# Keys projected first, their features turned to rows by DMA as pairs of float16, and the recall one block later

## The chip, the cores and the metric

The kernel runs on one core of a Trainium2 chip. The metric is the device time of that core in microseconds (us). TensorE (PE) multiplies matrices; ScalarE (ACT), VectorE (DVE) and GpSimd (POOL) work element by element; SyncE (SP) issues the DMA transfers. Each engine goes through its own instructions strictly in order, and waits where an input or a buffer isn't ready.

## What is computed

```python
o = g_beta * a_mem + (1 - g_beta) * a_dot      # per head, 32 heads of 18, 4 segments of 512 tokens
a_mem = phi(q) @ M / (phi(q) @ z + 1e-6)       # phi(t) = t + 1 if t > 0 else exp(t)
M = M + phi(k).T @ v ;  z = z + phi(k).sum()   # after each segment
a = o @ wo                                     # a_dot: causal softmax attention in the segment
b = (gelu(x @ w_gate) * (x @ w_up)) @ w_down   # 576 -> 4608 -> 576
out = g * a + (1 - g) * b                      # g = sigmoid(x . gate_w); x is 2048 x 576
```

## The kernel before

**Numbers as pairs.** A float32 operand is split into a high and a low float16 word with a common scale, and a product is three float16 matmuls (high by high, high by low, low by high). Making a pair takes one ACT instruction for the high words and one DVE instruction for the low words: lines L109 and L112 for weights, L170 and L175/L180 for x.

**Stages.** The first stage projects x to queries, keys and values, and forms what the memory M adds. It goes through four segments s = 0 to 3. Then come 72 steps of the feed-forward part, with the attention's products among them, and last the output projection. The order of PE, ACT, DVE and POOL is the order in which the program is written, inside one block of manual scheduling; only SP's queue is ordered by the framework.

**Columns.** In each segment `project` (L460 to L466) makes nine blocks of 128 columns by 512 tokens in PSUM, each from 14 matmuls of 512 columns (`chain_w`, L322 to L325). The blocks 0 to 4 hold queries and 4 to 8 keys, so block 4 holds both. `put_columns` (L468 to L491) stands one block later in the program: ACT writes the block's high words to `stage` (L470). Where phi is wanted, ACT also makes relu and exp (L475, L476), DVE the other half of phi (L480), and POOL adds the two (L481). DVE writes the low words (L486), and a DMA stores the pair (L487). Four PSUM buffers take the blocks in turn, and `stage` has three buffers. In segment 0 phi is only wanted of the keys, blocks 4 to 8; in segment 3 only of the queries.

**What stands beside the columns.** `beside_products` (L737) puts other work between the blocks. In segment 0 these are the projection weights: block j makes the pair `wp` of block j + 2 and, to j = 4, a part of the values' weights `wv`. In segments 0 to 2 `next_x` prepares the x of the segment after it: squares on ACT at j = 2 and 3, their sum on PE at j = 4 (`scale_x`, L155, with six small DVE steps, L157 to L164, that end in `xis`), six small POOL steps with the scales that follow from it (`outscale`, L120 to L127), then the high words at j = 5 to 7 and the low words at j = 6 to 8.

**Rows.** From segment 1 on, the nine blocks are preceded by four blocks q of 128 tokens. `vrows` makes the values (`chain_x`, L332 to L335, from x and `wv`), ACT evicts them twice (float16 pairs L506, and float32 with a column of ones, `v32`, L508), and DVE makes the low words (L511). Between them lies the memory's part of the segment before, p = s - 1. `key_rows` (L566) turns phi of the keys to rows by six float32 transposes on PE (L571, L573) and two ACT evictions (L575, L576). `memorize` (L578) then multiplies those rows with `v32` in five float32 matmuls (L585) that add up in PSUM over the four blocks, and `keep_memory` (L588) adds the masked sum to `bd`. `recall` (L533) multiplies phi of the queries with `bd` in five float32 matmuls (L540).

**Tail.** `out_step` (L1364, L1369) makes the output projection from pairs that POOL prepares (L1357), in a written order of steps (L1458 and below); u counts pairs of 128-token blocks.

Of the kernel before, what the change touches and what calls it, by code (L numbers as in the profile page):

```python
# [18 lines left out]
P = 128  # L19
D = 576  # L20
F = 4608
H = 32
# [21 lines left out]
def kernel(ctx: ExitStack, tc: tile.TileContext, xs, wqk, wv, wo, wgu, wd, beta, out):  # L44
# [355 lines left out]
    with tc.tile_pool(name="prj", bufs=2, side="right", reuse_waits="tile") as pp:  # L400
        al = pp.tile([P, 4, 2], F32, name="al", bufs=1)
        nal = pp.tile([P, 4], F32, name="nal", bufs=1)
        usc = pp.tile([P, 1], F32, name="usc", bufs=1)
        mp = stay.enter_context(tc.tile_pool(name="ffn", bufs=2, reuse_waits="tile"))
# [5 lines left out]
        W, phi, vst, v32, kr, mem = {}, {}, {}, {}, {}, {}  # L410
        QG = ((0, 1), (2, 3), (4, 5), (6, 7), (8,))
# [5 lines left out]
        def load_qk(g):  # L417
            js = QG[g]
            a, b = js[0], js[-1] + 1
            sp.dma_start(raw_qk[:, a:b], wqk[a:b].rearrange("j p k n -> p j (k n)"))  # L420
# [39 lines left out]
        def project(s, j):  # L460
            w = W[j]
            i = j % 4
            pr = bank("G") if i == 0 else bank("U") if i == 3 else bank("st", 2)
            chain_w(pr, lambda k, a: w[:, a, k * P : (k + 1) * P], x16[s])
            return s, j, pr

        def put_columns(s, j, pr):
            hf, c = divmod(s, 2)  # L468
            st = pp.tile([P, 2, L], F16, name="stage", bufs=3)
            act.activation(st[:, 0], pr, AF.Copy, scale=2.0**-14)  # L470
            with_phi = (j <= 4 and s >= 1) or (j >= 4 and s <= 2)
            if with_phi:
                e = pp.tile([P, L], F32, name="expm", bufs=2)
                f = phi[s, j] = pp.tile([P, L], F32, name="phi", bufs=9)
                act.activation(e, pr, AF.Relu, scale=nal[:, s : s + 1])  # L475
                act.activation(e, e, AF.Exp, scale=-1.0)  # L476

            def rest():
                if with_phi:
                    dve.tensor_scalar(f, pr, al[:, s, 0:1], 0.0, OP.mult, OP.max)  # L480
                    (dve if j == 8 and s == 0 else pool).tensor_tensor(f, f, e, OP.add)  # L481
# [8 lines left out]
            if j == 8 and s < 3:  # L490
                held.append(words)  # L491

        def put_rows(s, q, b, pv, unit, a):

            hf, c = divmod(s, 2)
            t = 4 * c + q
            if b == 0:
                st = vst[s, q] = pa.tile([P, H, VC], F16, name="vstage", bufs=4)
                pool.memset(st[:, :, VC - 1 : VC], 1.0)
                if s <= 2:  # L500
                    v32[s, q] = pa.tile([P, H, MC], F32, name="v32", bufs=6)
                    pool.memset(v32[s, q][:, :, DH:], 1.0)
# [3 lines left out]
            act.activation(st[:, hs, 0:DH], p3, AF.Copy, scale=unit)  # L506
            if s <= 2:
                act.activation(v32[s, q][:, hs, 0:DH], p3, AF.Copy, scale=a)  # L508

            def rest():  # L510
                dve.scalar_tensor_tensor(st[:, hs, DH : 2 * DH], p3, unit, st[:, hs, 0:DH], OP.mult, OP.subtract)  # L511
# [54 lines left out]
        def key_rows(s, q):  # L566
            ka, kb = bank("st", 2), bank("V")
            tok = slice(q * P, (q + 1) * P)

            for i in range(4):  # L570
                pe.transpose(ka[:, i * P : (i + 1) * P], phi[s, 4 + i][:, tok], ident)  # L571
            for i, j in ((0, 8), (1, 4)):
                pe.transpose(kb[:, i * P : (i + 1) * P], phi[s, j][:, tok], ident)  # L573
            k = kr[s, q] = pa.tile([P, KT * P], F32, name="krow", bufs=2)
            act.activation(k[:, :448], ka[:, 64:], AF.Copy)  # L575
            act.activation(k[:, 448:], kb[:, :192], AF.Copy)  # L576

        def memorize(s, q):  # L578
            if q == 0:
                mem[s] = bank("U"), bank("pv")  # L580
            k, v = kr.pop((s, q)), v32.pop((s, q))
            for j, (a, w) in enumerate(SPANS):
                h0, h1 = HEADS[j]
                o = mem[s][j // 3][:, (j % 3) * 8 * MC : (j % 3) * 8 * MC + (h1 - h0) * MC]
                pe.matmul(o, k[:, a : a + P], v[:, h0:h1].rearrange("p h d -> p (h d)"),  # L585
                          start=q == 0 and j % 3 == 0, stop=q == 3 and j in (2, 4), skip_group_check=True)

        def keep_memory(s):  # L588
            ka, kb = mem.pop(s)
            n = 8 * MC  # L590
            for o, d, k in ((ka[:, : 3 * n], flat(bd[:, 0:3]), flat(bdm[:, 0:3])),
                            (kb[:, :n], bd[:, 3], bdm[:, 3]),
                            (kb[:64, n : n + n // 2], bd[:64, 4, : n // 2], bdm[:64, 4, : n // 2])):
                if s == 0:
                    dve.tensor_tensor(d, o, k, OP.mult)
                else:
                    m = pa.tile([P, KT * P], F32, name="krow", bufs=2)[: o.shape[0], : o.shape[1]]
                    dve.tensor_tensor(m, o, k, OP.mult)
                    dve.tensor_tensor(d, d, m, OP.add)
# [8 lines left out]
        with tc.manual_schedule(engines=ORDERED):  # L608
# [35 lines left out]
            ident = pp.tile([P, P], F32, name="ident", bufs=1)  # L644
            bd = pp.tile([P, KT, 8 * MC], F32, name="bd", bufs=1)
            pool.memset(bd[64:, KT - 1], 0.0)
            make_identity(nc, ident)
# [40 lines left out]
            def next_x(c, j):  # L688
# [6 lines left out]
                if j == 4:  # L695
                    scale_x(c)
                    for i in range(2):
                        outscale(c, i)
                if 5 <= j < 8:
                    high_x(c, j - 5)  # L700
# [37 lines left out]
            def beside_products(s, j):  # L738
                if s == 0:
                    if j < 7:  # L740
                        make_qk(j + 2)
                    if j == 1:
# [3 lines left out]
                        outscale(0, 1)  # L746
                    if j < 5:
# [46 lines left out]
            for s in range(4):  # L794
                p = s - 1
                if s:
                    for q in range(4):
# [6 lines left out]
                        if q:  # L804
                            key_rows(p, q - 1)
# [5 lines left out]
                        if p >= 1:  # L811
                            recall(p, q)
# [5 lines left out]
                    key_rows(p, 3)  # L818
# [37 lines left out]
    with tc.tile_pool(name="keep", bufs=2, side="right", reuse_waits="tile") as kp, ExitStack() as tail:  # L856
# [560 lines left out]
        with tc.manual_schedule(engines=ORDERED):  # L1417
# [39 lines left out]
            for u in range(NT):  # L1457
                if u + 2 < NT:  # L1458
                    steps = (0, 6), (1, 7), (1, 1), (0, 5), (1, 4), (1, 2), (0, 3)
                elif u + 1 < NT:  # L1460
                    steps = (0, 6), (1, 7), (1, 1), (0, 5), (1, 6), (0, 3)
                else:
                    steps = (0, 2), (0, 5), (0, 4), (0, 3)
                for i, p in steps:
                    out_step(u + i, p)
                    if u == NT - 1:
                        if p == 2:
                            store(2 * u, 0)
# [4 lines left out]
                        if p == 3:  # L1473
                            store(2 * u, 1)
                if u + 1 < NT:
# [48 lines left out]
```

## Time and profile before

| | |
|---|---|
| time, median of 3 runs | 1579.53 us (1579.09 to 1580.05) |
| the profiled execution's time | 1579.74 us |
| its span, first to last instruction | 1577.9 us |
| busy: PE / PE weight loads | 1571.2 us (100%) / 936.7 us (59%) |
| busy: DVE / ACT / POOL | 1134.3 (72%) / 1175.1 (74%) / 1210.6 us (77%) |
| first stage: columns of segment 0 | 26.25 to 54.54 us |
| rows and columns of segment 1 | 54.54 to 75.47 to 104.95 us |
| rows and columns of segment 2 | 104.95 to 130.31 to 159.79 us |
| rows and columns of segment 3 | 159.79 to 185.33 to 218.63 us |

The starts of the stages are those of PE's first instruction in each. A timeline's row has its start, its time from the first start to the last end of the instructions it groups, the engine, the line, the operation with output and inputs, the shape and the count, and in brackets the idle time ahead of it with what ended it. Where instructions are pipelined, the start of the next row and not the end of this one says how long a row held its engine.

### The profile page before, as it was taken

To read this page: it belongs to the slowest core of one execution; us is meant where nothing else is said; L and a number is where in the kernel's file an instruction comes from. 1 tells how busy PE (TensorE), PEld (TensorE's weight loads), DVE (VectorE), ACT (ScalarE), POOL (GpSimd) and SP (SyncE) were. 2 spreads that over 40 slices of the span, in tenths; PEclk is the share of its full clock that TensorE was granted. 3 is DMA by queue.
4 is the path that set the end of the run, shared out by engine and by line. 5 is a ranking of instruction groups with operands and counts; after the bars stand their busy time and mean duration, and the time that the engine had idled before them with its cause. 6 is when DMAs were issued, how large, how long until landed. Compare 5 with 4: busy or idle time off the path is not lost.

```text
span 1577.9 us, 32595 instructions
## 1 busy us (share of the span) xinstructions
PE 1571.2 (100%) x11864; PEld 936.7 (59%) x11864; DVE 1134.3 (72%) x2974; ACT 1175.1 (74%) x1996; POOL 1210.6 (77%) x1173
## 2 busy tenths in 40 slices
PE   9999999999999999999999999999999999999998
PEld 6666754555555555555555555555555555555576
DVE  6677784777777777777777777777777777776565
ACT  6666444888888888888888888888888888886421
POOL 3233756788888888898987888887879797788697
PEclk9999999999999999999999999999999999999999
DMA  6532442688888798979887899889898888774653
GB/s 243 199 125 87 140 136 75 103 130 127 130 136 137 126 141 138 137 123 141 127 137 128 136 132 138 134 133 151 132 138 129 143 128 138 128 130 86 136 112 129
DMA packets 472680, 209.87 MB, mean 133 GB/s; under 512 B 427672, under 2 KB 437400, under 8 KB 472008
## 3 DMA queue, kind: packets, MB, share of 16 engines
q1 hardware_dynamic: 472520, 207.80, 73.7%
q8 instruction: 93, 1.52, 0.4%
q14 instruction: 67, 0.55, 0.1%
HBM read 91.87 MB, written 27.26 MB: 75 GB/s over the span
## 4 chain that ended last, share of the span: by engine, by line
PE 91%; POOL 4%; ACT 2%; DVE 2%; issue 0%; DMA 0%; POOLq 0%; ACTq 0%; DVEq 0%
PE dn L1007 25%; PE U L1047 17%; PE V L1047 12%; PE G L1047 12%; PE pv L962 4%; PE U L1054 2%; PE st L322 2%; PE dn L332 2%; PE G L322 1%; PE V L1059 1%; PE G L1059 1%; PE st L915 1%; PE G L1054 1%; PE V L1054 1%; POOL pairg L1339 1%; PE U L322 1%
## 5 line engine op out<-in xcount | busy, mean ns | idle before, releaser
L942 POOL TENSOR_TENSOR ph<-pf,ph 128x512 f16<-128x512 f32 (+1 forms) x256 | 354.0, 1405 | 173.2 <-ACT ph L941 173.2
L1007 PE MATMUL dn<-paird,hh 128*128 128x288 f16 x3396 | 476.3, 286 | 0.0
L1047 PEld LDWEIGHTS <-pairg 128*128 128x128 f16 x3024 | 285.5, 98 | 304.1 <-issue 18.1
L1007 PEld LDWEIGHTS <-hh 128*128 128x128 f16 x3456 | 332.1, 98 | 153.4 <-issue 18.2
L1015 DVE SCALAR_TENSOR_TENSOR acc<-dn,ev,acc 128x288 f32<-128x288 f32 x534 | 274.2, 514 | 54.1 <-PE dn L1007 44.0
L931 ACT ACTIVATE pf<-pf,mb,esc 128x512 f32<-128x512 f32 (+3 forms) x512 | 292.9, 642 | 7.0 <-POOL ph L942 0.4
L1047 PE MATMUL U<-xt,pairg 128*128 128x512 f16 x864 | 210.0, 379 | 0.0
L1047 PE MATMUL G<-x,pairg 128*128 128x512 f16 x864 | 209.9, 379 | 0.0
L1034 POOL TENSOR_TENSOR hh<-gl,hh 128x512 f16<-128x512 f32 x144 | 164.5, 1163 | 18.4 <-ACT hh L1033 18.4
L303 POOL TENSOR_TENSOR pairg<-raw,pairg 128x640 f16<-128x640 f32 (+2 forms) x144 | 174.4, 1235 | 5.1 <-ACT pairg L299 5.1
L299 ACT ACTIVATE pairg<-raw 128x640 f16<-128x640 f32 (+2 forms) x144 | 89.9, 650 | 113.2 <-POOL raw L293 65.3
L941 ACT ACTIVATE ph<-pf 128x512 f16<-128x512 f32 (+1 forms) x256 | 172.4, 720 | 0.0
L1192 DVE COPY gl<-U 128x512 f32<-128x512 f32 x72 | 49.8, 692 | 167.2 <-POOL hh L1034 150.3
L918 DVE CUSTOM_DVE_ANT_0 pf<-st,mask 128x512 f32<-128x512 f32 (+1 forms) x256 | 157.1, 614 | 0.0
L268 POOL TENSOR_SCALAR raw<-raw,sc 128x640 f32<-128x640 f32 x72 | 136.0, 1902 | 0.0
L918 DVE CUSTOM_DVE_ANT_0 pf<-dn,mask 128x256 f32<-128x256 f32 (+1 forms) x192 | 67.1, 375 | 82.7 <-PE dn L915 82.1
L1037 ACT ACTIVATE gl<-gl,sc 128x512 f32<-128x512 f32 x144 | 96.6, 715 | 37.1 <-DVE gl L1215 19.3
L1047 PE MATMUL V<-xt,pairg 128*128 128x512 f16 x432 | 105.7, 381 | 0.0
L1047 PE MATMUL U<-x,pairg 128*128 128x512 f16 x432 | 105.0, 379 | 0.0
L1047 PE MATMUL V<-x,pairg 128*128 128x512 f16 x432 | 104.8, 378 | 0.0
L1033 ACT ACTIVATE hh<-gl 128x512 f16<-128x512 f32 x144 | 82.6, 616 | 16.4 <-DVE gl L1029 16.3
L962 PEld LDWEIGHTS <-pt 128*128 128x128 f16 x2560 | 83.4, 96 | 6.3
(305 smaller groups left out, 2642.6 us busy)
## 6 DMA issues: line engine op xcount, KB each, us to landing
raw<-in_wgu_dram SPq DMA_DIRECT2D x36, 640.0 KB
rawd<-in_wd_dram SPq DMA_DIRECT2D x36, 288.0 KB
qt<-qk SPq DMA_DIRECT2D x132, 72.0 KB
kt<-qk SPq DMA_DIRECT2D x132, 72.0 KB
qk<-stage SPq DMA_DIRECT2D x36, 256.0 KB
qt<-qk SPq DMA_DIRECT2D x132, 36.0 KB
kt<-qk SPq DMA_DIRECT2D x132, 36.0 KB
vp<-vstage SPq DMA_DIRECT2D x16, 296.0 KB
```

The costliest lines, as they stand in the source:

```text
L268: pool.tensor_scalar(r, r, scl[f // 2][0][:, 0:1], None, OP.mult)
L303: pool.tensor_tensor(spot(f, *p, 1), raw_g[f][:, p[0] : p[1]], spot(f, *p, 0), OP.subtract)
L918: dve.tensor_tensor_reduce(prob[a][:, COL[qi] : COL[qi + 1]], out[qi], mask[:, L - (qi + 1) * P :], 1.0, -3e38, OP.add, OP.max, mx[a][:, q ...
L931: act.activation(r, r, AF.Exp, bias=b[:, qi : qi + 1], scale=esc[:, 0, c : c + 1])
L941: act.activation(h[:, 0, cols], p[:, cols], AF.Copy)
L942: pool.tensor_tensor(h[:, 1, cols], p[:, cols], h[:, 0, cols], OP.subtract)
L962: pe.matmul(ov, pr[:, 10 * i + COL[qi] // P + kb], v[:, 4 * e + kb, c0 : c0 + VC], start=kb == 0 and i == 0, stop=kb == qi and i == 1)
L1007: pe.matmul(o[:, :NH], hh[:, a, q * P : (q + 1) * P], w[:, b, n * NH : (n + 1) * NH], start=i == 0, stop=i == 5)
L1015: dve.scalar_tensor_tensor(av, o[:, :NH], ev, av, OP.mult, OP.add)
L1034: pool.tensor_tensor(hh[:, 1], t, hh[:, 0], OP.subtract)
L1037: act.activation(t, o, AF.Gelu_apprx_tanh, scale=scl[f // 2][0][:, 2 + c : 3 + c])
L1047: pe.matmul(o, w[:, i, (a + k) * P : (a + k + 1) * P], x[:, b + k], start=start and k == 0 and i == 0 and b == h, stop=k == 1 and i == 1, ...
```

## The change

Everything but the tail's order lies in the first stage.

- **Keys first.** `JO` sets the order of the blocks to 4, 5, 6, 7, 8, 0, 1, 2, 3, in segments 0 to 2; the weights' loads are grouped to match. Segment 3 keeps queries first.
- **Scaled features.** New `key_scales` makes per-segment factors from the outscale, with five POOL steps and one DVE step that POOL waits for. It stands behind `outscale` at j = 4 (for segment 0 at j = 1). For the key blocks 5 to 8 phi is formed scaled: DVE's half takes the scaled factor, and a new POOL instruction multiplies the exp half by it, ahead of the add.
- **Pairs.** New `key_pairs` makes `kpair` of each key block, one block later: an ACT copy to float16 and a POOL subtraction (for block 4 an ACT copy with a scale and a DVE instruction). Two DMA transposes of 128 x 512 from SP write each pair to `krows`, 30 in all.
- **Memorize in float16.** `key_rows` (72 PE transposes, 24 ACT evictions) and `v32` (24 ACT evictions and its memsets) are gone. `memorize` takes 15 float16 matmuls of 76 to 152 (or 72 to 144) columns a block in place of 5 in float32, with the values' own pairs; their low words stand ahead of the high ones now. `keep_memory` takes nine small DVE steps a segment in place of three to six.
- **Recall one block later**, the last one beside the first columns. Buffers: phi 9 to 7, `vstage` 4 to 6.
- **Tail.** In the last two rounds steps that don't need the latest pair come ahead of those that do.

```diff
+        JO = (4, 5, 6, 7, 8, 0, 1, 2, 3)
+        QG = ((0, 1), (2, 3), (4,), (5, 6), (7, 8))
...
+        def key_scales(s):
+            m = kfz[:, s : s + 1]
+            v = pp.tile([P, 1], F32, name="kv", bufs=2)
+            pool.tensor_scalar(m, al[:, s, 0:1], 2.0**30, 1.0, OP.mult, OP.max)
+            dve.tensor_scalar(v.bitcast(I32), m.bitcast(I32), EXP, None, OP.bitwise_xor)
+            pool.tensor_scalar(kf[:, s : s + 1], v, 2.0**13, None, OP.mult)
+            pool.tensor_scalar(kal[:, s : s + 1], kf[:, s : s + 1], al[:, s, 0:1], None, OP.mult)
+            pool.tensor_scalar(kfd[:, s : s + 1], m, al[:, s, 1:2], None, OP.mult)
+            pool.tensor_scalar(m, m, 2.0**-14, None, OP.mult)
...
+        def key_pairs(s, j):
...
+            if j == 4:
+                kr[s] = pa.tile([P, 2, 4, KT * P], F16, name="krows", bufs=1)
+                act.activation(h[:, 0], f, AF.Copy, scale=kf[:, s : s + 1])
+                dve.scalar_tensor_tensor(h[:, 1], f, kf[:, s : s + 1], h[:, 0], OP.mult, OP.subtract)
+            else:
+                act.activation(h[:, 0], f, AF.Copy)
+                pool.tensor_tensor(h[:, 1], f, h[:, 0], OP.subtract)
+            for i in range(2):
+                sp.dma_start(kr[s][:, i, :, (j - 4) * P : (j - 3) * P], h[:, i], transpose=True)
...
                 act.activation(e, e, AF.Exp, scale=-1.0)
+            if to_rows:
+                key_pairs(*to_rows.pop(0))
...
-                    dve.tensor_scalar(f, pr, al[:, s, 0:1], 0.0, OP.mult, OP.max)
-                    (dve if j == 8 and s == 0 else pool).tensor_tensor(f, f, e, OP.add)
-                if j < 8 or s == 3:
+                    keys = j > 4
+                    dve.tensor_scalar(f, pr, kal[:, s : s + 1] if keys else al[:, s, 0:1], 0.0, OP.mult, OP.max)
+                    if keys:
+                        pool.tensor_scalar(e, e, kf[:, s : s + 1], None, OP.mult)
+                    pool.tensor_tensor(f, f, e, OP.add)
+                    if j >= 4 and s <= 2:
+                        to_rows.append((s, j))
...
             for j, (a, w) in enumerate(SPANS):
                 h0, h1 = HEADS[j]
-                pe.matmul(o, k[:, a : a + P], v[:, h0:h1].rearrange("p h d -> p (h d)"),
+                for n, (i, c) in enumerate(((0, DH), (1, DH), (0, 0))):
+                    pe.matmul(o[:, :, :DH] if c == 0 else o, k[:, i, 64 + a : 64 + a + w],
+                              v[:, h0:h1, c : c + MC if c else DH],
...
                 elif u + 1 < NT:
-                    steps = (0, 6), (1, 7), (1, 1), (0, 5), (1, 6), (0, 3)
+                    steps = (0, 6), (1, 1), (0, 5), (1, 2), (0, 3)
                 else:
-                    steps = (0, 2), (0, 5), (0, 4), (0, 3)
+                    steps = (0, 6), (0, 7), (0, 5), (0, 4), (0, 3)
```

ACT in the columns of segment 0, before: from the third block on to the fifth. `stage` is a block's high words, `wp` and `wv` are weights' high words, `pairg` takes the squares of the next segment's x, and G, U and st are PSUM buffers.

```order
L149 ACTIVATE pairg<-raw 128x512 x3
L470 ACTIVATE stage<-st 128x512
L109 ACTIVATE wp<-acc,wsc 128x640
L109 ACTIVATE wv<-acc,wsc 128x578
L149 ACTIVATE pairg<-raw 128x512 x2
L470 ACTIVATE stage<-U 128x512
L109 ACTIVATE wp<-acc,wsc 128x640
L109 ACTIVATE wv<-acc,wsc 128x578
L470 ACTIVATE stage<-G 128x512
```

The same engine after, from the fourth block on; L496 is the new copy of the block ahead to float16, and the last rows lie beside the fifth block.

```order
L504 ACTIVATE stage<-U 128x512
L509 ACTIVATE expm<-U,nal 128x512
L510 ACTIVATE expm<-expm 128x512
L496 ACTIVATE kpair<-phi 128x512
L109 ACTIVATE wp<-acc,wsc 128x640
L109 ACTIVATE wv<-acc,wsc 128x578
L504 ACTIVATE stage<-G 128x512
L509 ACTIVATE expm<-G,nal 128x512
L510 ACTIVATE expm<-expm 128x512
L496 ACTIVATE kpair<-phi 128x512
L109 ACTIVATE wp<-acc,wsc 128x640
L170 ACTIVATE x_556<-raw,xsc 128x1024
```

Each of the first five blocks now has relu, exp and, from the second on, a copy between its high words and the weights that a later block is projected with.

POOL at the place of the fourth and fifth block of segment 0, before: the outscales of segment 1, and behind them the features of segment 0.

```order
L120 TENSOR_SCALAR al<-wis,xis 128x1
L123 TENSOR_SCALAR nal<-al 128x1
L124 TENSOR_SCALAR esc<-al 128x1
L125 TENSOR_SCALAR esc<-esc 128x1
L120 TENSOR_SCALAR al<-wis,xis 128x1
L127 TENSOR_SCALAR gha<-gh,al 128x32
L481 TENSOR_TENSOR phi<-phi,expm 128x512 x4
```

After: the same outscales, from the last of them on, with what follows; the four `kf` are the new scales, `kv` is DVE's part of them.

```order
L127 TENSOR_SCALAR gha<-gh,al 128x32
L476 TENSOR_SCALAR kf_98<-al 128x1
L478 TENSOR_SCALAR kf_96<-kv 128x1
L479 TENSOR_SCALAR kf_97<-kf_96,al 128x1
L480 TENSOR_SCALAR kf_99<-kf_98,al 128x1
L481 TENSOR_SCALAR kf_98<-kf_98 128x1
L519 TENSOR_SCALAR expm<-expm,kf_96 128x512
L520 TENSOR_TENSOR phi<-phi,expm 128x512
L497 TENSOR_TENSOR kpair<-phi,kpair 128x512
L519 TENSOR_SCALAR expm<-expm,kf_96 128x512
```

The features of the fourth key block stand behind outscales and scales that belong to the next segment, and the subtraction, which needs ACT's copy, stands ahead of the next block's multiply.

More of the change, by code (lines that the diff above doesn't have):

```diff
@@ L403 @@
         usc = pp.tile([P, 1], F32, name="usc", bufs=1)
+        kf, kal, kfz, kfd = (pp.tile([P, 3], F32, name=f"kf{i}", bufs=1) for i in range(4))
         mp = stay.enter_context(tc.tile_pool(name="ffn", bufs=2, reuse_waits="tile"))
@@ L564, in put_recall @@
             sp.dma_start(oms[hf][t * P : (t + 1) * P, :], mo)
[L566 to L576, printed above, removed]
         def memorize(s, q):
@@ L746, in beside_products @@
                         outscale(0, 1)
+                        key_scales(0)
                     if j < 5:
@@ L810 @@
                         behind_rows(s, q)
-                        if p >= 1:
-                            recall(p, q)
+                        if p >= 1 and q:
+                            recall(p, q - 1)
                         pv = vrows(s, q, 1)
```

75 lines of the change are left out of this document (41 added, 34 removed).

## The prediction

> **What bounds the kernel now.** I read the page first: the span, the busy times, the granted clock in 40 slices and the chain that ended last.
>
> ```profile
> span 1577.9 us, 32595 instructions
> PE 1571.2 (100%) x11864; PEld 936.7 (59%) x11864; DVE 1134.3 (72%) x2974; ACT 1175.1 (74%) x1996; POOL 1210.6 (77%) x1173
> PEclk9999999999999999999999999999999999999999
> PE 91%; POOL 4%; ACT 2%; DVE 2%; issue 0%; DMA 0%; POOLq 0%; ACTq 0%; DVEq 0%
> ```
>
> PE is busy for all but 6.7 us and holds 91% of the chain. So PE work taken away counts in full, if nothing makes PE wait instead. The profiled execution took 1579.74 us, 1.8 more than its span and 0.2 more than the median of 1579.53. About 0.2%, or 3.2 us, is what a measurement can tell from no change.
>
> Next I read PE's timeline of the two places that are edited: a block of rows in segment 2, and segment 0's columns.
>
> ```profile
> 107.88 1.64 PE L332 MATMUL dn<-wv,x 128*128 128x290 f16 x12
> 109.36 0.29 PE L334 MATMUL dn<-wv,x 128*128 128x290 f16 x1
> ...
> 111.32 0.60 PE L571 MATMUL st<-ident,phi 128*128 128x128 f32 x4
> 111.75 0.38 PE L573 MATMUL V<-ident,phi 128*128 128x128 f32 x2
> 111.97 1.54 PE L540 MATMUL st<-bd,phi 128*128 128x152 f32 x10
> ...
> 115.08 0.94 PE L585 MATMUL U<-v,krow 128*128 128x152 f32 x6
> 115.85 0.60 PE L585 MATMUL pv<-v,krow 128*128 128x152 f32 x4
> 116.29 1.63 PE L332 MATMUL dn<-wv,x 128*128 128x288 f16 x12
> ```
>
> ```profile
> 38.35 2.75 PE L322 MATMUL G<-x,wp 128*128 128x512 f16 x12
> ...
> 41.37 1.24 PE L155 MATMUL dn<-pairg,onesb 128*128 128x512 bf16 x5
> 42.45 2.75 PE L322 MATMUL st<-x,wp 128*128 128x512 f16 x12
> ...
> 51.52 2.75 PE L322 MATMUL G<-x,wp 128*128 128x512 f16 x12
> ...
> 54.54 1.63 PE L332 MATMUL dn<-wv,x 128*128 128x288 f16 x12
> ```
>
> A column takes 3.02 us (51.52 to 54.54), and no row has a wait in brackets: PE goes from block to block. Columns are counted n = 0 to 8 in the order in which they are projected.
>
> **The gain, on PE.** The six transposes go: 111.32 to 111.97, 0.65 us a block. `memorize` took 115.08 to 116.29, 1.21 us. Twelve float16 matmuls of 290 columns take 1.48 us (107.88 to 109.36), 0.425 ns a column each; the fifteen new ones have 2016 columns together, 0.86 us. So a block falls by 0.65 + 1.21 - 0.86 = 1.00 us, and twelve blocks by 12.0. The values' words now come with gaps between the heads, which no row here shows in a moving operand: if that costs what float32 did, 1.21 stays and the gain here is 7.8; I take 0.86, since the float16 row is of the same kind of words. In the tail PE stood once for a pair:
>
> ```profile
> 1566.69 0.66 PE L1364 MATMUL pv<-wo,x 128*128 128x288 f16 x4 [1.02 <-POOL x L1357]
> ```
>
> The new order puts other steps into that wait: -1.0. The gain is 13.0 us. The recall is only moved. The 48 evictions that go are on ACT, the nine DVE steps of `keep_memory` are wanted some 27 us later, by the next rows: both zero, as long as ACT and DVE wait for PE in those stages.
>
> **The loss, in segment 0's columns.** These rows, of ACT, DVE and POOL in that stage and POOL's outscales in segment 1's, price the steps; a row's duration is its latency, the difference of two starts what it holds its engine.
>
> ```profile
> 32.22 0.58 ACT L470 ACTIVATE stage<-G 128x512 f16<-128x512 f32 x1
> 32.69 0.82 ACT L109 ACTIVATE wp<-acc,wsc 128x640 f16<-128x640 f32 x1
> 33.41 0.77 ACT L109 ACTIVATE wv<-acc,wsc 128x578 f16<-128x578 f32 x1
> ...
> 35.94 1.66 ACT L149 ACTIVATE pairg<-raw 128x512 bf16<-128x512 f32 x3
> ...
> 42.75 0.69 ACT L475 ACTIVATE expm<-G,nal 128x512 f32<-128x512 f32 x1
> 43.47 0.63 ACT L476 ACTIVATE expm<-expm 128x512 f32<-128x512 f32 x1
> 44.00 0.81 ACT L109 ACTIVATE wp<-acc,wsc 128x640 f16<-128x640 f32 x1
> ```
>
> ```profile
> 42.54 0.82 DVE L112 SCALAR_TENSOR_TENSOR wv<-acc,wsc,wv 128x578 f16<-128x578 f32 x1
> 43.28 0.69 DVE L157 TENSOR_REDUCE x<-dn 128x1 f32<-128x512 f32 x1
> ...
> 44.69 0.14 DVE L164 TENSOR_SCALAR xis<-xv 128x1 f32<-128x1 f32 x1
> ...
> 45.35 0.88 DVE L112 SCALAR_TENSOR_TENSOR wp<-acc,wsc,wp 128x640 f16<-128x640 f32 x1
> 46.14 0.75 DVE L480 TENSOR_SCALAR phi<-G,al 128x512 f32<-128x512 f32 x1
> ```
>
> ```profile
> 47.26 1.28 POOL L481 TENSOR_TENSOR phi<-phi,expm 128x512 f32<-128x512 f32 x1
> ```
>
> ```profile
> 94.67 0.29 POOL L120 TENSOR_SCALAR al<-wis,xis 128x1 f32<-128x1 f32 x1 [5.09 <-DVE xis L164]
> ...
> 96.39 4.71 POOL L481 TENSOR_TENSOR phi<-phi,expm 128x512 f32<-128x512 f32 x3
> ```
>
> Three operations are new, and the page's groups have their nearest rows:
>
> ```profile
> L1034 POOL TENSOR_TENSOR hh<-gl,hh 128x512 f16<-128x512 f32 x144 | 164.5, 1163 | 18.4 <-ACT hh L1033 18.4
> L268 POOL TENSOR_SCALAR raw<-raw,sc 128x640 f32<-128x640 f32 x72 | 136.0, 1902 | 0.0
> L1033 ACT ACTIVATE hh<-gl 128x512 f16<-128x512 f32 x144 | 82.6, 616 | 16.4 <-DVE gl L1029 16.3
> ```
>
> The copy is 0.62 us, the subtraction 1.16, and POOL's multiply by columns 1.90 x 512/640 = 1.5 (between 1.28, an add's, and 1.9). The five steps of `key_scales` take 1.5, at 0.29 each (six outscales: 94.67 to 96.39), with DVE's one within 0.1 beside.
>
> In before ACT gave the first four columns only their high words; now the first five need stage, relu, exp and copy: 0.47 + 0.72 + 0.53 + 0.52 = 2.24 us, ahead of 0.72 + 0.67 for weights. That is 3.63 us, more than PE's 3.02, before the squares. The copy stands ahead of the weights and waits for POOL's add. I follow it in steps:
>
> (a) Column 4's weights. ACT starts column 0 at 32.22; stage, relu, exp and the high word of W3 end at 34.75, of wv at 35.4; DVE then has W3's low word, four small steps and wv's low word (to about 37.2), column 0's half of phi (37.9); POOL adds (39.2), ACT copies (39.8), high word 0.82, low word 0.88: 41.5. PE is there at 38.35: **3.2 late**.
>
> (b) Squares. After that high word (ACT free at 40.5) come wv 0.67, three squares 1.6, stage, relu, exp and copy 2.24, W5 0.72, wv 0.67, two squares 1.1: 47.5. Column 4 has ended at 44.5: the sum L155 waits **3.0**, and ends at 48.6.
>
> (c) Column 7. ACT goes on from 47.5 with column 3's stage, relu, exp, the copy (2.24), W6 and wv: 51.2. DVE's wv low ends at 52.1, and `xis` comes 1.55 later (43.28 to 44.83), 53.6. POOL then does outscales 1.7, scales 1.5, column 3's multiply 1.5 and add 1.28: 59.6. ACT's copy 0.62, W7's high word 0.82 and low word 0.88: 61.9. PE has only columns 5 and 6 in between, 48.6 + 6.04 = 54.6: **7.3 late**.
>
> (d) Column 8. From the copy's end, 60.2: subtraction 1.16, multiply 1.5, add 1.28, copy 0.62, weights 1.70, to 66.5; column 7 ends at 64.9: **1.6 late**.
>
> Together +15.1. Were (a) and (b) hidden, (c) would still take 1.55 + 1.7 + 1.5 + 1.5 + 1.28 + 0.62 + 1.70 = 9.85 against 6.04, so 3.8, and (d) 1.6: the floor is +5.4. I take the walk, since each step of it is a row and an order.
>
> **The loss at the start of rows 2 and 3.** In segments 1 and 2 the chain ends not at weights but at the next x, whose words stand behind the copies:
>
> ```profile
> 94.55 1.15 ACT L170 ACTIVATE x<-raw,xsc 128x1024 f16<-128x1024 f32 x1 [0.72 <-DVE xsc L163]
> ...
> 100.11 2.07 DVE L175 SCALAR_TENSOR_TENSOR x<-raw,xsc,x 128x1024 f16<-128x1024 f32 x1
> ```
>
> From the end of L155: 1.55, outscales 1.7, scales 1.5, multiply and add 2.8, copy 0.6 make 8.2; subtraction, multiply, add and the next copy 4.6: 12.8; x's second high words 1.15 and low words 2.07: 16.0. PE has four columns and a part of the first values' block, 12.1 + 0.7 = 12.8, so it waits 3.2, and 1.3 more for the third part behind DVE's two steps of a column: 4.5 each, +9.0 for both. At best the copies come in time: 0.
>
> Segment 3's rows have fewer columns behind them; 0, up to 3.
>
> **Transposes.** They leave PE for SP's queue, 30 of 128 x 512. The nearest row is ten squares in one, these have four:
>
> ```profile
> L948 SPq DMA_TRANSPOSE pt<-ph x256: 1252/1694/4665, 283.4 to 1446.0; - x128
> ```
>
> So 0.5 to 1.9 us of SP each, 0.7 by the middle; a pair of 1.4 hides under a column of 3.02. Rows are first read some 10 us after the last copy: 0 taken, and the stores behind them on SP are paid in a rival.
>
> The Trainium skill (VectorE: DVE Perf Modes, "The three transpose paths") has 1309 ns by DMA and 390 ns by TensorE for 128 x 128, and advises TensorE where PSUM may take the result, which speaks against this change. By it a pair of transposes would be an estimated 8 x 1.31 = 10.5 us one behind the other; rival 4 is what that does here. The row above has 125 to 169 ns a square on SP, beside 109 ns on PE, so the sum doesn't follow the page.
>
> **The sum.** 1579.7 - 13.0 + 15.1 + 9.0 = 1590.8, so 1590.6 against the median: **1591**.
>
> **Rivals.**
>
> 1. The waits are hidden: faster. If POOL's small steps and multiply run well below their rows, the copy is never the last input of ACT and PE keeps its pace; 1579.7 - 13.0 = 1566.7. It needs (c)'s 9.85 under 6.04. Against it: 4.5 of the 9.85 is POOL by rows. 10%.
> 2. Only the floor of segment 0: 1566.7 + 5.4 = 1572, and to 1578 with part of the later waits. For it: ACT is idle in many places of this stage and the starts may come earlier than I walk. 20%.
> 3. The transposes run at the top of their row, 1.9 on SP; 3.8 a pair over 3.02 holds `stage`'s three buffers and the loads behind. In segment 0 DMA is busy already:
>
> ```profile
> 24.00:54.00 30.00, 30.00 (x140) 13.87 (x139) 26.88 (x50) 23.70 (x41) 8.35 (x14) 1.00 0.77 261
> ```
>
> The ninth column is the DMA's share, 0.77. Fifteen pairs at 0.8 over: +12, 1603. 8%.
> 4. The transposes land too late for `memorize`. If each takes the row's longest, 4.7, and they go one by one, five pairs are 47 us; from the first copy at 40 the last lands at 87, where the rows' first `memorize` comes some 10 us after they start at 69: +8 in each segment, 24, 1615. The page's 10.5 a pair gives 52 us and, by the same count, an estimated +13 each, 1630. 2%.
> 5. The clock falls in the long waits. Every slice of PEclk is 9, and no row of before has PE idle for over 3 us behind the start, so the trace can't say. If after (c), and after two waits of 4.5, PE ran at half its clock for one column's time, each would cost 1.5: +4.5, 1595. The Trainium skill (TensorE: Matmul & The Clock Gate, "Part 1") says that one idle window of about 3.4 us halves it and a busy window restores it; a 3.4 us window at half speed would cost an estimated 1.7. 10%.
>
> **How the numbers follow.** My forecast has 50% (1584 to 1600). Faster by over 3.2 us: rival 1 and half of rival 2 and nothing else, 0.19. Within 3.2: the other part of rival 2, less than all of it, 0.08. Slower: the rest, 0.73. The range leaves out rival 1 and the lower half of rival 2's, and takes in rivals 3 and 5: 1574 to 1604; the forecast's own is 1584 to 1600.
>
> **What would show it.** Right: PE's L322 rows of segment 0 carry waits in brackets ended by DVE `wp` L112, the longest of about 7 us ahead of column 7, and L155 one for ACT's squares; rows 1 begin near 69 us in place of 54.54; L332 rows at the start of rows 2 and 3 wait for `x` L175/L180; a rows block is 1.0 us shorter; the tail's 1.02 is gone. Wrong: no such waits (rival 1); waits that end at `krows` or `stage` (rivals 3 and 4); PEclk under 9 (rival 5); or `memorize` above 0.86 us a block.

## The result, and the profile after

The changed kernel takes 1606.69 us, the median of five runs (1606.32 to 1606.87), against 1579.53 (1579.09 to 1580.09) for the kernel before on the same chip: a ratio of 1.0171, interval 1.0156 to 1.0186. It is 27.2 us slower. 1591 was forecast; the direction came out, the size did not. The profiled execution took 1606.87, with a span of 1605.1.

The page of the changed kernel: span, busy times, granted clock.

```profile
span 1605.1 us, 32640 instructions
PE 1574.6 (98%) x11852; PEld 927.2 (58%) x11852; DVE 1137.5 (71%) x2991; ACT 1166.6 (73%) x1963; POOL 1250.5 (78%) x1199
PEclk9898899999999999999999999999999999999999
```

PE was idle for 6.7 us and is now idle for 30.5, and the clock row has slices under 9, all in the first stage. The starts of the stages in the two timelines give where the time went; the forecast by stage is the prediction's own terms.

| stage | before | after | change | forecast |
|---|---|---|---|---|
| up to segment 0's columns | 26.25 | 26.06 | -0.2 | 0 |
| columns of segment 0 | 28.29 | 47.02 | +18.7 | +15.1 |
| rows of segment 1 | 20.93 | 18.36 | -2.6 | -3.65 |
| rows of segment 2 | 25.36 | 31.56 | +6.2 | +0.85 |
| rows of segment 3 | 25.54 | 31.57 | +6.0 | +0.85 |
| columns of segments 1 to 3 together | 92.26 | 92.21 | 0 | -1.05 |
| feed-forward part and tail | 1359.27 | 1358.32 | -1.0 | -1.0 |

PE's timeline of segment 0's columns, after: the rows that wait. In brackets stands the idle time ahead of the row, and what ended it.

```profile
41.63 0.77 PE L322 MATMUL G<-x,wp 128*128 128x512 f16 x2 [3.31 <-ACT wp L109]
42.55 3.70 PE L322 MATMUL G<-x,wp 128*128 128x512 f16 x10 [0.15 <-DVE wp L112]
...
47.99 0.90 PE L155 MATMUL dn<-pairg,onesb 128*128 128x512 bf16 x2 [0.66 <-ACT pairg L149]
...
63.91 1.03 PE L322 MATMUL U<-x,wp 128*128 128x512 f16 x2 [7.33 <-ACT wp L109]
65.10 4.36 PE L322 MATMUL U<-x,wp 128*128 128x512 f16 x10 [0.16 <-DVE wp L112]
```

The waits stand where steps (a), (b) and (c) had them, ended by what those steps named; 3.2, 3.0 and 7.3 were forecast. Step (d)'s wait ahead of column 8 doesn't show. What was not forecast: a column starts as soon as the high words are there and then stands for the low words, and its matmuls are slow, ten in 3.70 or 4.36 where twelve took 2.75.

ACT and POOL ahead of that wait, after:

```profile
62.50 0.63 ACT L496 ACTIVATE kpair<-phi 128x512 f16<-128x512 f32 x1 [7.55 <-POOL phi L520]
63.04 0.81 ACT L109 ACTIVATE wp<-acc,wsc 128x640 f16<-128x640 f32 x1
```

```profile
56.06 0.30 POOL L120 TENSOR_SCALAR al<-wis,xis 128x1 f32<-128x1 f32 x1 [2.98 <-DVE xis L164]
...
59.54 1.59 POOL L519 TENSOR_SCALAR expm<-expm,kf 128x512 f32<-128x512 f32 x1
61.21 1.26 POOL L520 TENSOR_TENSOR phi<-phi,expm 128x512 f32<-128x512 f32 x1
```

ACT stands 7.55 at the key copy, with the high words of W7, column 7's weights, queued behind it. POOL was idle until `xis`; outscales and scales take 56.06 to 59.54, 3.5 us, then come multiply and add.

The start of segment 2's rows, after:

```profile
120.92 0.90 PE L332 MATMUL dn<-wv,x 128*128 128x288 f16 x6
125.12 0.66 PE L332 MATMUL dn<-wv,x 128*128 128x288 f16 x2 [3.30 <-ACT x L170]
126.44 1.14 PE L332 MATMUL dn<-wv,x 128*128 128x288 f16 x4 [0.66 <-DVE x L175]
129.34 0.42 PE L334 MATMUL dn<-wv,x 128*128 128x288 f16 x1 [1.76 <-DVE x L180]
...
129.80 3.11 PE L332 MATMUL dn<-wv,x 128*128 128x290 f16 x12
```

Three waits, 5.7 us, for the next x's words, and behind them twelve matmuls in 3.11 in place of 1.64. The windows show the clock of two such places (the last numbers of a row are granted clock, DMA share and GB/s):

```profile
63.90:69.70 5.80, 5.63 (x14) 1.82 (x15) 2.85 (x4) 3.29 (x5) 4.98 (x5) 0.54 0.37 90
...
130.00:133.00 3.00, 3.00 (x15) 1.86 (x13) 2.38 (x5) 1.42 (x3) 2.79 (x4) 0.50 0.94 344
```

And a block of rows, with `memorize` in float16:

```profile
81.00 0.81 PE L612 MATMUL U<-vstage,krows 128*128 128x152 f16 x9
81.64 0.60 PE L612 MATMUL pv<-vstage,krows 128*128 128x152 f16 x6
82.18 1.64 PE L332 MATMUL dn<-wv,x 128*128 128x288 f16 x12
```

81.00 to 82.18 is 1.18 us a block, where 0.86 was forecast and 1.21 stood before.

From here on the theory was: the chains of the prediction hold, and the 16 us beyond it are the half clock behind the waits (some 12) and `memorize` (12 x 0.32 = 3.8). The rivals: the slow matmuls cost nothing of themselves, and the copies' place is not what holds the weights, but POOL's own load or ACT's.

### The profile page after: what moved, and what is told of

Its sections match the earlier page's. It is cut to its first block, busy times and chain, and to the rows that moved or that the text cites. A ratio compares the mean times of both kernels' runs of the same rounds, so it can differ in the third digit from the quotient of the medians.

```text
span 1605.1 us, 32640 instructions
## 1 busy us (share of the span) xinstructions
PE 1574.6 (98%) x11852; PEld 927.2 (58%) x11852; DVE 1137.5 (71%) x2991; ACT 1166.6 (73%) x1963; POOL 1250.5 (78%) x1199
## 4 chain that ended last, share of the span: by engine, by line
PE 89%; POOL 3%; ACT 2%; DVE 2%; issue 1%; DMA 1%; SPq 0%; POOLq 0%; ACTq 0%; DVEq 0%
PE dn L1041 26%; PE U L1081 17%; PE V L1081 12%; PE G L1081 11%; PE pv L996 4%; PE U L1088 2%; PE dn L332 2%; PE V L1093 1%; PE G L1093 1%; PE st L949 1%; PE st L1398 1%; POOL phi L520 1%; PE G L1088 1%; PE V L1088 1%; PE dn L949 1%
```

## The experiments

### PE kept busy in the waits

`warm(n)` issues n matmuls of 128 columns whose result is not read.

```diff
+                    if s == 0 and j in (4, 7):
+                        warm(40 if j == 4 else 100)
                     pr = project(s, j)
...
+                        if s > 1 and q == 0:
+                            warm(45)
                         pv = vrows(s, q, 0)
```

> The changed kernel with small matmuls whose result nobody reads, put ahead of columns 4 and 7 of segment 0 (40 and 100 of 128 columns) and ahead of the rows of segments 2 and 3 (45 each), where PE waits. The waits stay, only PE is not idle in them. If the half clock behind each long wait costs what the trace seems to say (1.7 + 2.6 + 0.3 in segment 0, some 3.5 at each start of rows), the granted clock is 1.00 throughout and the time falls by 8 to 11, to 1596 to 1599. Rival: the slow matmuls behind a wait come from inputs that are still late, and the clock costs nothing of itself: 1606.7, within 1.

1607.81, ratio 1.018 (1.0165 to 1.0196): nothing gained. So the theory that the clock costs 12 fell. Of segment 0's columns 4, 7 and 8 in this kernel:

```profile
42.87 2.33 PE L322 MATMUL G<-x,wp 128*128 128x512 f16 x10 [0.32 <-DVE wp L112]
...
64.21 0.60 PE L322 MATMUL U<-x,wp 128*128 128x512 f16 x2 [1.73 <-ACT wp L109]
65.41 2.33 PE L322 MATMUL U<-x,wp 128*128 128x512 f16 x10 [0.59 <-DVE wp L112]
...
69.58 0.60 PE L322 MATMUL G<-x,wp 128*128 128x512 f16 x2 [1.41 <-ACT wp L109]
70.78 4.02 PE L322 MATMUL G<-x,wp 128*128 128x512 f16 x10 [0.59 <-DVE wp L112]
```

Columns 4 and 7 do run at full speed now, and PE then waits for column 8's weights instead; the slow column is the last one. In segment 0 the weights set the pace, and a slow column in front of a later wait costs nothing: column 8's low words are there 44.4 us after the stage's start with column 7 slow (70.42 from 26.06) and 44.3 with it fast (70.72 from 26.39). The stage takes 48.7 here in place of 47.0, because now its last column is the slow one. In the rows PE still went idle in three pieces after the added matmuls, so that part had not been tested; a later kernel does it.

### Key copies one step later

```diff
-            if to_rows:
-                key_pairs(*to_rows.pop(0))
...
                     beside_products(s, j)
+                    if to_rows:
+                        key_pairs(*to_rows.pop(0))
                     finish_later()
```

> The changed kernel with the key copy, its subtraction and its transposes issued one step later in the same column, behind the weights' and the next x's words in place of ahead of them. Nothing else is moved. If the copy that waits for POOL holds up the words queued behind it on ACT, the waits ahead of column 7 (7.3) and at the starts of rows 2 and 3 (5.7 and 4.9) go, and the half clock with them: 1571 to 1578, faster than before. Rival: five more ACT steps and the POOL chain are simply too much for a column's 3.02, wherever they stand: the waits stay by half or more, 1590 or above. A second rival: without the waits the transposes (2.5 a pair on SP) come too close: waits that end at krows or stage, 1580 to 1588.

1601.00, ratio 1.0137 (1.0122 to 1.0152): a gain of 5.7, much less than the theory's 30. PE and ACT in segment 0:

```profile
56.09 5.18 PE L322 MATMUL U<-x,wp 128*128 128x512 f16 x12 [4.00 <-DVE stage L525]
```

```profile
60.78 0.63 ACT L496 ACTIVATE kpair<-phi 128x512 f16<-128x512 f32 x1 [6.20 <-POOL phi L518]
```

W7's high words now come at 53.5, but the copy still stands 6.20 for POOL, ahead of column 8's weights. What ends PE's wait is DVE's low words of column 3 (L525, 55.36 to 56.04): they release the PSUM buffer that column 7 takes, and stand on DVE behind `key_scales`' step, which waits 2.09 for POOL. Moving the copy past one step only changed whose words it holds.

### Scales at the end of the segment

```diff
                 if j == 4:
                     scale_x(c)
-                    for i in range(2):
-                        outscale(c, i)
-                    if c < 3:
-                        key_scales(c)
...
                 if j == 8:
+                    for i in range(2):
+                        outscale(c, i)
+                    if c < 3:
+                        key_scales(c)
```

> The changed kernel with the outscales and the key scales of the next segment moved on POOL from the fifth column to the end of the ninth, behind the key features. If they lie on the chain as the prediction's step (c) has it, 3.5 go from the wait ahead of column 7 and from each start of rows, with a part of the half clock: 1592 to 1597. Rival: POOL is not what the copy waits for, 1606.7 within 1.

1597.91, ratio 1.0116 (1.0099 to 1.0133): 8.8 less. The wait ahead of column 7 is 3.32 where it was 7.33. Of the three waits at the start of segment 2's rows, 3.30, 0.66 and 1.76, the first is gone, and 0.86 and 2.23 are left. Segment 0's columns take 43.0 in place of 47.0, the rows of segments 2 and 3 2.9 and 2.3 less. The scales did lie on the chain, with about the 3.2 that step (c) priced (3.5 in the trace); 1597.9 is 0.9 above the range given.

### Both moves, and then DVE in POOL's place

The two edits above together:

> Both moves at once: the key copies one step later in their column, and the next segment's outscales and key scales at the end of the ninth column. Alone they gave 5.7 and 8.8. If the two hold up different words, the gains add: 1591 to 1593. If the scales were what made the moved copy still wait, more: 1580 to 1588. Rival: POOL's own loop of subtraction, multiply and add (4.0 a key column against 3.02) is the bound, and the second move adds little to the first: 1595 to 1598.

1592.47, ratio 1.0082 (1.0069 to 1.0096): 14.2 less than the change, where the two alone give 14.5. They add. Segment 0's columns take 35.1 (25.55 to 60.67). The last words of x for segment 2:

```profile
115.73 0.42 PE L334 MATMUL dn<-wv,x 128*128 128x288 f16 x1 [4.70 <-DVE x L180]
```

On top of it, in segments 1 and 2, the pairs without POOL:

```diff
             if j == 4:
                 kr[s] = pa.tile([P, 2, 4, KT * P], F16, name="krows", bufs=1)
+            if j == 4 or s:
                 act.activation(h[:, 0], f, AF.Copy, scale=kf[:, s : s + 1])
                 dve.scalar_tensor_tensor(h[:, 1], f, kf[:, s : s + 1], h[:, 0], OP.mult, OP.subtract)
...
-                    keys = j > 4
+                    keys = j > 4 and s == 0
```

> The version with both moves (copies one step later, scales at the end), and in segments 1 and 2 all pairs as block 4's: scale by ACT's copy, low words by DVE, no multiply and no subtraction on POOL. Left there were waits of 4.7 at the starts of rows 2 and 3 for x's last words, behind copies that waited 2.5 each for POOL. If POOL's loop of 4.0 and more a key column is what is left there, both waits go: 1592.5 - 8 to 9 = 1584. Rival: the copy's place on ACT ahead of the next column holds it, whoever makes the pair: within 2 of 1592.5.

1585.26, ratio 1.0037 (1.0023 to 1.0051): another 7.2.

```profile
113.60 0.30 PE L334 MATMUL dn<-wv,x 128*128 128x288 f16 x1 [1.91 <-DVE x L180]
```

4.70 became 1.91, the rows of segments 2 and 3 take 25.8 and 26.4, and the granted clock is 1.00 over the whole span. What is left above the kernel before is 5.7: segment 0's columns still take 35.1, 6.9 too much.

The same edit in all segments, on the changed kernel without the moves:

> The changed kernel with all key blocks made as block 4 is: no multiply on POOL, the scale taken by ACT's copy, and the low words by DVE in place of POOL's subtraction. POOL is left with one add a column in place of 4.0 us. If POOL's loop sets the copies' times, 1.6 go from the wait ahead of column 7, 2.8 from column 8 and some 4 from each start of rows: 1592 to 1597. Rival: DVE, already busy for 26.9 of 30 us in segment 0, takes POOL's place there: 1601 or above.

1600.36, ratio 1.0135 (1.0121 to 1.0149), between the two forecasts. The rows of segment 2 wait less, but

```profile
61.33 5.30 PE L322 MATMUL U<-x,wp 128*128 128x512 f16 x12 [5.71 <-DVE kpair L495]
```

in segment 0 DVE is where column 7's wait ends. POOL is relieved and DVE takes part of its place.

### Memorize's columns

The moving operand is a dense tile of ones, with dense columns in PSUM; then half of them from a segment's second block on. What is summed is then not the memory; these two kernels serve for the time alone. The edit for the dense one:

```diff
-                    pe.matmul(o[:, :, :DH] if c == 0 else o, k[:, i, 64 + a : 64 + a + w],
-                              v[:, h0:h1, c : c + MC if c else DH],
+                    pe.matmul(o[:, : (h1 - h0) * DH] if c == 0 else o, k[:, i, 64 + a : 64 + a + w],
+                              kept["dense"][:, : (h1 - h0) * (MC if c else DH)],
```

> The changed kernel with memorize's moving operand a dense tile of ones, and dense columns in PSUM, with the same number of matmuls, weights and columns; the memory is then a sum of features and not of features by values. If the gaps between the heads make the fifteen matmuls take 1.18 a block in place of the 0.86 that the columns give, a block falls to 0.86 and the time by 3.8, to 1602.9. Rival: each matmul has a floor of its own (its weight load), the gaps cost nothing: 1.18 a block, 1606.7 within 0.6.

> The kernel with the dense tile of ones, with half the columns in memorize's matmuls for the blocks after a segment's first; what is summed there is incomplete. Dense columns took 1.09 a block in place of 1.18. If a matmul of this kind has a floor of about 72 ns whatever its columns (its weights being loaded), a block stays at 1.0 to 1.1. Rival: time by columns, 0.55 to 0.6 a block.

1606.01 (ratio 1.0169, 1.0154 to 1.0185) and 1601.33 (1.0139, 1.0121 to 1.0158). A block of the dense kernel, and one with half the columns:

```profile
80.79 0.74 PE L611 MATMUL U<-dense,krows 128*128 128x152 f16 x9
81.37 0.58 PE L611 MATMUL pv<-dense,krows 128*128 128x152 f16 x6
81.88 1.64 PE L332 MATMUL dn<-wv,x 128*128 128x288 f16 x12
```

```profile
85.51 0.47 PE L611 MATMUL U<-dense,krows 128*128 128x76 f16 x9
85.81 0.47 PE L611 MATMUL pv<-dense,krows 128*128 128x76 f16 x6
86.21 1.03 PE L332 MATMUL dn<-wv,x 128*128 128x288 f16 x7
```

Dense takes 1.09: the gaps cost 0.09, not 0.32. The first nine matmuls go by columns: 0.58, and 0.30 with half of them. The last six take 0.51 and still 0.40, where their columns would give 0.29 and 0.14: neither forecast's floor for all of them nor time by columns. Three of those six have weights of 64 columns in place of 128 and stand last; what exactly costs the 0.2 there is open.

### The tail alone

The change's hunk of the tail, on the kernel before:

> The kernel before with the new order of the tail alone. The wait of 1.02 ahead of the step that needs the latest pair goes: 1.0 less than before, ratio 0.9994. Rival: another step waits in its place, 0 within 0.2.

1578.26 against 1579.42, ratio 0.9994 (0.9985 to 1.0003). The interval can't tell it from no change. The traces can: that wait of 1.02 is in no row of the tail any more, here or after the change, and the part behind the first stage is 1.0 shorter.

### The clock, in the rows

```diff
+            gaps = {2: 52, 6: 10, 8: 28} if s > 1 and (q, b) == (0, 0) else {}
...
+                if i in gaps:
+                    warm(gaps.pop(i))
```

> The changed kernel with matmuls that nobody reads in the three waits of the first values' block of segments 2 and 3 (52, 10 and 28 of 128 columns), so that PE is busy until the last of x's words is there. If the half clock behind these waits costs time of itself, the two blocks that follow run at full speed and each start gains 2.3: 1602. Rival: the next words set the pace and the clock costs nothing: 1606.7 within 1.

1603.83, ratio 1.0155 (1.0141 to 1.0169): 2.9 less than the change, where 1602 was forecast. Segment 2's rows, and a row of segment 3's:

```profile
129.80 0.30 PE L334 MATMUL dn<-wv,x 128*128 128x288 f16 x1 [0.69 <-DVE x L180]
...
130.06 1.64 PE L332 MATMUL dn<-wv,x 128*128 128x290 f16 x12
...
193.12 0.39 PE L91 MATMUL dn<-stat,ones 128*128 128x10 f32 x2 [1.59 <-ACT junk L86]
```

x's last words come at the same place, and behind them the blocks run at full speed. The rows of segment 2 take 29.23 in place of 31.56, those of segment 3 30.49 in place of 31.57: the half clock cost 2.3 and 1.1. In segment 2 nothing later was waited for, and the loss counted in full; in segment 3 PE, now faster, waits 1.59 for ACT at L91, where the changed kernel has no wait, so a part of the loss was hidden.

### Pairs in the rows

Queries first again; pairs and transposes made in the next rows, where ACT and POOL have room, and `memorize` beside the second column:

```diff
-        JO = (4, 5, 6, 7, 8, 0, 1, 2, 3)
+        JO = (0, 1, 2, 3, 4, 5, 6, 7, 8)
...
                         put_rows(s, q, 1, *pv)
-                        if q:
-                            memorize(p, q - 1)
+                        for _ in range(2 if q == 3 else 1):
+                            key_pairs(*to_rows.pop(0))
...
-                    if s and j == 0:
-                        memorize(p, 3)
+                    if s and j == 1:
+                        for q in range(4):
+                            memorize(p, q)
```

> The changed kernel's arithmetic in the order of the kernel before: queries first again, the key pairs and their transposes made in the next segment's rows (one a block, two in the last), all four blocks of memorize beside that segment's second column; phi has 9 buffers, vstage 8, kpair and mo one each. If the loss is only that the pairs stand ahead of weights and x in the columns, nothing of it is left: PE's saving of 12 x 0.68 and the tail's 1.0 remain, 1579.5 - 9.2 = 1570, with up to 5 for new waits: 1570 to 1575. Rival: the pairs cost POOL, ACT and DVE too much anywhere, or the transposes land too late for memorize: 1580 or above.

1616.63, ratio 1.0242 (1.0228 to 1.0256). To fit, this version had one buffer for the pairs and one for `mo`, and both were waited for:

```profile
85.76 0.31 PE L610 MATMUL pv<-vstage,krows 128*128 128x152 f16 x1 [2.71 <-DMA krows<-kpair]
...
201.71 2.70 PE L574 MATMUL st<-bd,phi 128*128 128x152 f32 x10 [8.92 <-DVE mo L596]
```

With two of each (the idle exp buffers take the pairs), and two pairs in the first block:

> The version with the pairs in the rows again, with two buffers for the pairs (the exp buffers, idle there) and two for mo in place of one each, and the blocks' pairs split as two, one, one, one. In the first version copies stood 3 to 4 for the transposes of the pair ahead, memorize waited for krows, and rows of segment 3 stood 8.9 for mo. If that was the one buffer each, the waits go: rows as in before less the transposes, 1570 to 1576, faster than before. Rival: pairs, transposes and stores are one chain on SP and POOL that doesn't fit into the rows: memorize waits for krows still, 1582 or above.

1592.22, ratio 1.0077 (1.0063 to 1.009). Segment 0's columns take 28.3 again, and `memorize` waits for nothing; `mo` is still waited for, 1.77 and 2.19 at the longest. And

```profile
72.33 2.78 PE L332 MATMUL dn<-wv,x 128*128 128x288 f16 x12 [3.45 <-DVE vstage L545]
```

the values' evictions now stand on ACT behind copies that wait, 4.61 for the transposes of an earlier pair. So both forecasts, 1570 to 1575 and 1570 to 1576, failed: in each of the three places tried the copy held what was queued behind it. No version tried is faster than the kernel before by more than the tail's 1.0.

## Why the prediction was right in direction and wrong in size

**The gain.** The transposes' 0.65 a block went as forecast, and the tail's 1.0 too. `memorize`'s step failed: "I take 0.86, since the float16 row is of the same kind of words" took one end of a range whose other end, 1.21, was nearly the truth. It was 1.18. That is 3.8 of the miss, and the gaps named as the risk were only 0.09 a block of it. Of the some 16 us by which the change came out slower than forecast, 3.6 lie in segment 0's columns and 8.6 in the rows of segments 2 and 3.

**Segment 0.** The waits of (a), (b) and (c) came where they were forecast, (b)'s as 0.66 in place of 3.0, since column 4 ended at 46.5 and not at 44.5. (d)'s shows only where column 7 runs at full speed: 1.41 and 0.59 in the kernel with `warm`, where 1.6 stood. That L155's end, forecast at 48.6, came at 48.7 is in part luck: ACT's squares ended 0.9 later than in step (b), but three of the five matmuls had been done ahead of them.

The total was 18.7 where 15.1 stood, and W7's low words ended at 65.0 and not at 61.9. Two steps put a wait at nothing. Step (a) has POOL add column 0's halves by 39.2, but segment 0's own `key_scales` was in the way: DVE stood 0.69 for POOL in it, POOL was at it until 38.8, and the add ended at 40.1:

```profile
38.83 1.26 POOL L520 TENSOR_TENSOR phi<-phi,expm 128x512 f32<-128x512 f32 x1
40.07 1.59 POOL L519 TENSOR_SCALAR expm<-expm,kf 128x512 f32<-128x512 f32 x1
...
47.24 2.15 POOL L519 TENSOR_SCALAR expm<-expm,kf 128x512 f32<-128x512 f32 x1
```

Step (c) has ACT go on through the copy behind column 3's exp without a wait; it stood 1.04 there:

```profile
51.22 0.63 ACT L496 ACTIVATE kpair<-phi 128x512 f16<-128x512 f32 x1 [1.04 <-POOL phi L520]
```

The third term is the price of steps that overlap on POOL and DVE; the rows that gave the low words' price have no large POOL step beside them:

```profile
40.89 0.75 DVE L494 SCALAR_TENSOR_TENSOR kpair<-phi,kf,kpair 128x512 f16<-128x512 f32 x1 [1.88 <-ACT kpair L493]
...
46.78 1.16 DVE L112 SCALAR_TENSOR_TENSOR wp<-acc,wsc,wp 128x640 f16<-128x640 f32 x1 [2.31 <-ACT wp L109]
47.87 1.24 DVE L112 SCALAR_TENSOR_TENSOR wv<-acc,wsc,wv 128x578 f16<-128x578 f32 x1
```

The multiply was put at 1.5 and the low words at 0.88 and 0.82. So `xis` came at 55.96 and not at 53.6: 0.9 from step (a), 1.0 from the copy's wait and some 0.4 from slower low words, which also delayed the add that the copy waited for. The other 0.7 to W7's low words are outscales and scales, multiply and low words, each a little slower than its price. Step (a) also left out DVE's low words of block 4's pair (L494), but W4's high words came only at 41.6, by when those were done, so this cost nothing.

The Trainium skill (GPSIMD Engine Reference, the table's row on SBUF interfaces) says that GpSimd shares them with VectorE and that they collide when a DVE instruction has two SBUF inputs. The rows agree in part: L112, with two, took 1.16 beside POOL's subtraction, four times, and L517, with one input from PSUM, stays at 0.74. But L494, with two, kept 0.75 beside multiplies of 1.57 to 1.59, three times.

**Rows 2 and 3.** Forecast 4.5 each on top of the gains; without `memorize`'s part they came out 4.4 and 4.2 above that. 2.3 and 1.1 of it are the clock, by the kernel that kept PE busy; the prediction had it as a rival and not as a term. Most of the rest is x's words. PE goes on with the last of them 8.4 and 7.6 behind the start of the rows, and the twelve matmuls ahead take 1.5 of that (104.95 to 106.42 in the kernel before): 6.9 and 6.1 late, where 4.5 stood. In segment 3 the 1.59 for ACT belongs to it too. DVE and POOL, after:

```profile
125.10 1.28 DVE L175 SCALAR_TENSOR_TENSOR x<-raw,xsc,x 128x1024 f16<-128x1024 f32 x1 [3.27 <-ACT x L170]
...
127.67 1.61 DVE L180 SCALAR_TENSOR_TENSOR x<-raw,xsc,x 64x512 f16<-64x512 f32 x1
```

```profile
119.42 2.60 POOL L519 TENSOR_SCALAR expm<-expm,kf 128x512 f32<-128x512 f32 x1
...
125.22 3.52 POOL L520 TENSOR_TENSOR phi<-phi,expm 128x512 f32<-128x512 f32 x2
```

The second low words end at 126.4, 17.6 behind the end of L155 (its matmuls start at 107.75 and hold PE for 1.08) where 16.0 was forecast, and the third 2.9 after those, where 1.3 stood. `xis` came at 110.5, but POOL was still at the subtraction of the block ahead and began the outscales at 111.1. POOL's multiply took 2.60 beside x's low words, two adds 3.52 together, and the third low words 1.61, where they took 0.73 with POOL idle (at 73.94). The prices of overlap, in both places, are read from the trace; no kernel took the overlap alone away.

**The rivals.** The waits did not hide (rival 1), nor was it only the floor (rival 2): the kernels with moves show the links of the chain by what each move gave. The transposes held next to nothing (rivals 3 and 4), though a pair took 2.5 on SP in place of 1.4:

```profile
L499 SPq DMA_TRANSPOSE krows<-kpair x30: 1189/1216/1366, 40.9 to 185.5; - x30
```

That is 0.30 a square. The Trainium skill's 1309 ns for a 128 x 128 transpose by DMA (VectorE: DVE Perf Modes, "The three transpose paths") would have been four times that, and `memorize` never waited for `krows` after the change. One sign of rival 3 was there: at 77.81 ACT had stood 5.97 for a store of `stage` (1.29 in the kernel before), and PE stood 0.68 behind it at 79.27; how much of that the transposes did, no run separates. The clock (rival 5) was real, 2.9 us by the kernel that took it away from the rows, in place of 4.5. It came on top of the forecast and not instead of it, and the range had little room for that: 1604 was its end.

## What to carry to other kernels

A conversion that waits for a slow engine costs what is queued behind it on its own in-order engine; moved one step, it holds the next words instead. Before putting such work ahead of something that feeds PE, follow one turn of the whole loop (here subtraction, multiply and add on POOL: 4.0 us and more against a column of 3.02), and price steps that will overlap on POOL and DVE with rows in which both are busy. Where a bound has two ends and the operation isn't in the trace, the sum should be given with both, and several small misses in one direction added up in the range.

## What the runs showed of the hardware

- Behind waits of 3.3 us and more PE ran at a granted clock of about half for some 4 to 6 us (0.54 and 0.50 in the windows above). It followed also after shorter gaps in a row: 1.73, 0.59, 1.41 and 0.59, with a column between them, and then ten matmuls in 4.02. Gaps of 0.71 and 0.59 alone did not bring it (column 6 of the changed kernel, ten in 2.33). The Trainium skill (TensorE: Matmul & The Clock Gate, "Part 1") has one idle window of about 3.4 us as the cause; those gaps, none of which is that long, show that PE busy for part of the time was not enough either.
- The loss from a slow clock depended on what was waited for next: nothing for column 7 of segment 0, 2.3 in segment 2's rows, and 1.1 in segment 3's, where a wait of 1.59 took its place.
- Nine dense float16 matmuls of 152 or 144 columns took 64 ns each, with half the columns 33 ns; with gaps of one head's words between heads 71 ns.
- Beside POOL some DVE instructions with two SBUF inputs took longer: L112 1.16 and 1.24 in place of 0.88 and 0.82, L180 1.61 in place of 0.73. L494, also with two, kept 0.75. POOL's multiply went from 1.59 to 2.15 or 2.60.
